# A held weight load and an earlier one: expert 1's second matrix waits for a store, expert 2's loads go out one group sooner

## The chip, the cores and the metric

The kernel runs on one core of a Trainium2 chip. The metric is the time of one execution on the device, in microseconds. Three runs of the kernel before took 1010.5, 1010.03 and 1009.81 us; their median is 1010.03 us.

The core has five engines, each of which takes its instructions in a fixed order: TensorE (PE, matmuls and transposes into the eight banks of PSUM), VectorE (DVE), ScalarE (ACT), GpSimd (POOL) and SyncE (SP, which here only issues transfers). Transfers go through 16 DMA engines, which two queues of this kernel feed at the same time: those that SP issues (the profile's q1, hardware_dynamic) and those that GpSimd issues (q0, software_dynamic).

## The reference

An attention with feature maps feeds a mixture of eight experts. Cut to what matters:

```python
def phi(x):
    proj = einsum('bhsd,df->bhsf', x, w_phi)
    proj = proj - max(abs(proj), axis=-1, keepdims=True)
    return concatenate([exp(proj), exp(-proj)], axis=-1)
q_p, k_p = phi(q), phi(k)
kv, z = einsum('bhsf,bhsd->bhfd', k_p, v), sum(k_p, axis=2)
x = (q_p @ kv) / (q_p @ z + 1e-06)          # then reshaped to 4608 x 512

P = exp(x @ w_gate - max)                    # 4608 tokens x 8 experts
for _ in range(8):
    P /= P.sum(1, keepdims=True) + 1e-09
    P /= P.sum(0, keepdims=True) + 1e-09
    P *= N / E
for e in range(8):
    out += P[:, e:e + 1] * (maximum(x @ w1[e], 0) @ w2[e])
```

Every token goes through every expert; w1[e] is 512 x 1024 and w2[e] 1024 x 512, each 2 MB in float32 and 1 MB in bfloat16 on the chip.

## The kernel before, in words

The program is written as a list of operations with what each reads, writes and which buffers it takes. A planner (class `Plan`, line 199) gives each engine its order: it models durations, buffers and both DMA queues (class `Links`, line 127, in which a transfer has a speed of its own and gets a share when both queues are busy), and starts whatever can start first; among operations that can start at the same moment the one written first goes first. The order that comes out is what the engines execute. So a change of a dependency, or of where a call stands in the text, can move instructions on every engine.

**Stages.** From 0 to about 204 us runs the attention. It leaves x in SBUF, transposed, as `xT`: 4608 tokens in nine groups of 512. Then run the routing (`routing`, line 1146: eight rounds that alternate on VectorE between row sums and column sums, with one small matmul against `colw` a round on TensorE, line 622 in the profile) and, at the same time on TensorE, the up and down products of expert 0. From about 244 us on come experts 1 to 7, whose products use Strassen-Winograd sums: seven products instead of eight, with sums of blocks formed beforehand on VectorE (`sub`, line 1236; all of these have line 1240 in the profile).

**Sums of x.** For expert 1 `sums_x` (line 1428) forms them per pair of groups: three sums X[3], X[2], X[4] and, because experts 2 to 7 use one more level for three of the products, `fine_x` (line 1365) forms four more for each of the blocks "11", "21" and "t1". All are stored to DRAM by SP: `xd` (X[n], line 1422), `xp` (a block that needs no sums, line 1450), and `xi` or `xi0t`, `xi2t`, `xi4t`, `xi6t` (the fine blocks; two parts straight from `xT`, lines 1369 and 1371, and the four sums in one store of 256 KB, line 1385). Experts 2 to 7 read them back (`load_fine`, line 1389).

The ring "X" has four buffers (line 492). X[3], X[2] and X[4] of the pair keep three of them until expert 1's product has read them. The fourth is taken in turn by the sums of "11", "21" and "t1" and then by the first sum of the next pair: VectorE can't write the next ones until the store of the last has landed. VectorE takes everything else, the rounds of the routing among it, behind these subtractions in its order. SP has eight semaphores for its transfers, used in turn, and so issues a transfer only when the eighth before it has landed.

**Weights.** `load_w` (line 514) has GpSimd issue two transfers, w1[e] and then w2[e], each 2 MB read and 1 MB written, with a cast. There are two places for each matrix: `wx`, which the attention uses until it ends, and one that expert 0 uses. Expert 1's loads wait for the key "late", the end of the attention. Those of expert e > 1 wait also for `("acc", 4, 0, 0)`: the first quarter of the accumulator of group 4, so that they stand on GpSimd behind the accumulation that writes it in the expert before. Expert 1's w2 is read by `sums_down`, called at the end of its second unit, and by its down products.

**The expert loop** (line 1979). Each expert goes through the pairs (0,1), (2,3), (4,5), (6,7) and the group 8. The down product of a group (`down7`, line 1791) runs in the units of the groups behind it. It forms sums of the hidden tile on VectorE (`hx<-hs`, line 1240), multiplies, and adds P times the result to `acc`: in part on VectorE (line 1860), in part on ScalarE (line 1872) and then GpSimd (line 1875, three accumulations for a group, in the order in which the down products come). `up7` (line 1480) finishes hidden tiles with an add and a relu on VectorE (line 1530 for expert 1) and on ScalarE (line 1535); one PSUM bank carries several products in turn, so that the next may start only when the add or read of the last is done.

Of the kernel before, what the change touches and what calls it, by code (L numbers as in the profile page):

```python
# [349 lines left out]
def kernel(  # L350
# [11 lines left out]
    nc = tc.nc  # L362
# [32 lines left out]
    acc = [accp.tile([128, 4, DD], FP32, name=f"acc{g}", tag=f"acc{g}") for g in range(NA)]  # L395
# [12 lines left out]
    late = {}  # L408
# [19 lines left out]
    def dma(queue, nbytes, rate, fn, r=(), w=()):  # L428

        speed, unit = LINK.get(rate, (rate, 40))  # L430
        if nbytes == 2 << 20:
            speed, unit = 400, 150
        o = plan.op(queue, 0.8 if queue == "POOL" else 0.6, 0.0, fn, r, w, (), nbytes / speed)
        o.turn, o.unit = rate == 148, unit

    TI, GR, KM, QM, PM, NM, RM = 0, 0, 0, 0, 0, 0, 0
    R = {}
# [68 lines left out]
    def new(tag):  # L506
        return R[tag].new()
# [3 lines left out]
        return buf().bitcast(BF16)  # L511


    def load_w(e, r=()):
        w1, w2 = new("w1"), new("w2")
        for w, src in ((w1, moe_w1), (w2, moe_w2)):
            dma("POOL", 2 << 20, 280, lambda w=w, src=src: nc.gpsimd.dma_start(
                out=w(), in_=src[e].rearrange("(c p) f -> p c f", p=128)),
                r, [(w, i, j) for i in range(2) for j in range(2)])
        return w1, w2  # L520

    def load_w0(i, r):
# [508 lines left out]
    for b in range(2):  # L1031
# [4 lines left out]
        w=["wphi_f0"])  # L1036
    dma("ACT", 1 << 15, 100, lambda: nc.scalar.dma_start(out=wphi_f[64:128, :], in_=w_phi),
        w=["wphi_f1"])
# [13 lines left out]
    for i in range(2):  # L1052
        dve(450, lambda i=i: nc.vector.memset(vrd[i], 0.0),
            w=[("vrd", i, h, *y) for h in range(2) for y in ((), (1,))])
# [79 lines left out]
    o = plan.op("X", 0.0, 0.0, swap, w=["late"])  # L1134
# [101 lines left out]
    def sub(eng, el, out_, x, y, op, r, w):  # L1236
        f = nc.vector if eng is dve else nc.gpsimd
        kw = {"shared": True} if eng is dve else {}
        eng(el * 0.5 if eng is dve else el * 1.04 + 128,
            lambda: f.tensor_tensor(out=out_(), in0=x(), in1=y(), op=op), r, w, **kw)  # L1240

    def sums_up(e, w1):

        def q(i, j):
            return lambda: w1()[:, 2 * j:2 * j + 2, 512 * i:512 * i + 512]

        S = [None] + [new("T") for _ in range(3)]

        def s(n):
            return lambda: S[n]().rearrange("p (a b) -> p a b", a=2)  # L1250


        a11, a12, a21, a22 = (1, 0), (1, 1), (0, 0), (0, 1)
        late = ["late"] + (["P"] if e == 1 else [])

        def k(a):
            return [(w1, *a)]

        sub(dve, 1024, s(2), q(*a11), q(*a21), ALU.subtract, k(a11) + k(a21) + late, [S[2]])
        sub(dve, 1024, q(*a21), q(*a21), q(*a22), ALU.add, k(a22) + late, k(a21))  # L1260
        sub(dve, 1024, s(1), q(*a21), q(*a11), ALU.subtract, k(a21) + k(a11) + late, [S[1]])
        sub(dve, 1024, s(3), q(*a12), s(1), ALU.subtract, k(a12) + [S[1]] + late, [S[3]])
        A = {"11": (q(*a11), k(a11)), "12": (q(*a12), k(a12)), "22": (q(*a22), k(a22)),
             "s1": (q(*a21), k(a21)), "s2": (s(1), [S[1]]), "s3": (s(2), [S[2]]),
             "s4": (s(3), [S[3]])}
        if e > 1:
            for n in INNER:
                fine_up(A, n)
        return A
# [48 lines left out]
    def xq(gs, i, j):  # L1318

        n = len(gs)  # L1320
        return lambda: xT[:, 2 * i:2 * i + 2, 512 * gs[0]:512 * (gs[0] + n)].rearrange(
            "p k (a b) -> p a k b", a=n)[:, :, :, 256 * j:256 * j + 256]

    def xall(gs):
        return [k for g in gs for k in xkeys(g)]
# [12 lines left out]
    class Turns:  # L1338
# [4 lines left out]
        def next(self):  # L1343
# [16 lines left out]
    Xi = {(g[0], n): dram.tile([128, 7, 256], BF16, name=f"xi{g[0]}{n}")  # L1360
          for g in pairs for n in INNER.values()}
# [3 lines left out]
    def fine_x(gs, n, b, r0):  # L1365

        g = gs[0]
        r = xall(gs) + ["late", *r0]
        dma("SP", 1 << 16, 160, lambda: nc.sync.dma_start(
            out=Xi[g, n][:, 0, :], in_=b()[:, 0, 0, :]), r, [("Xi", g, n, 0)])  # L1370
        dma("SP", 1 << 17, 160, lambda: nc.sync.dma_start(
            out=Xi[g, n][:, 1:3, :], in_=b()[:, :, 1, :]), r, [("Xi", g, n, 1)])
        y = new("X")

        def t(n):
            return lambda: y().rearrange("p a k c -> p (a k) c")[:, n]

        def blk(k, a):
            return lambda: b()[:, a, k, :]

        sub(dve, 256, t(0), blk(0, 1), blk(0, 0), ALU.subtract, r, [(y, 0), "order of X"])
        sub(dve, 256, t(2), blk(1, 1), blk(0, 1), ALU.subtract, r, [(y, 2)])
        sub(dve, 256, t(1), blk(1, 1), t(0), ALU.subtract, [*r, (y, 0)], [(y, 1)])
        sub(dve, 256, t(3), blk(1, 0), t(1), ALU.subtract, [*r, (y, 1)], [(y, 3)])
        dma("SP", 1 << 18, 160, lambda: nc.sync.dma_start(
            out=Xi[g, n][:, 3:7, :], in_=y().rearrange("p a k c -> p (a k) c")),
            [(y, i) for i in range(4)], [("Xi", g, n, 2)])

# [27 lines left out]
    def new_x():  # L1416
        return {n: new("X") for n in (2, 3, 4)}
# [10 lines left out]
    def sums_x(gs, r0=()):  # L1428

        X = new_x()  # L1430

        def x(n):
            return lambda: X[n]()[:, 0:len(gs)]

        b11, b12, b21, b22 = (xq(gs, *ij) for ij in ((0, 1), (0, 0), (1, 1), (1, 0)))
        el, keys = 512 * len(gs), xall(gs)
        r = keys + ["late", *r0]
        sub(dve, el, x(3), b22, b12, ALU.subtract, r, [X[3], "order of X"])
        sub(dve, el, b12, b12, b11, ALU.subtract, ["late", *r0], keys)
        sub(dve, el, x(2), b22, b12, ALU.subtract, r, [X[2]])  # L1440
        sub(dve, el, x(4), b21, x(2), ALU.subtract, r + [X[2]], [X[4], "order of X"])
        for n in (3, 2, 4):
            move_x(gs, n, True, X)
        if len(gs) == 2:
            for n, b in (("22", b22), ("11", b11), ("21", b21), ("t1", b12)):
                if n in INNER.values():
                    fine_x(gs, n, b, r0)
                else:
                    for a in range(2):
                        dma("SP", 1 << 17, 160, lambda n=n, a=a, b=b: nc.sync.dma_start(  # L1450
                            out=Xp[gs[0], n][:, a], in_=b()[:, a]), r, [("Xp", gs[0], n, a)])
        return X
# [524 lines left out]

    early, dn = [plain(8)], plain(7)
    for e in range(1, E):
        w1, w2 = load_w(e, ["late", ("acc", 4, 0, 0)] if e > 1 else ["late"])  # L1980
        if e == 1:
            nextX = sums_x(pairs[0])
        A7 = sums_up(e, w1)
        B7 = sums_down(e, w2) if e > 1 else None
        turn = [*pairs, (8,)] if e < E - 1 else [(8,), *pairs]
        if e == 2:
            o = plan.op("X", 0.0, 0.0, lambda: None, w=["K"])
            for d in plan.ops[:-1]:
                if any(b.ring is R["X"] for b in d.bufs):
                    d.users.append(o)  # L1990
                    o.deps.append(d)
                    o.left += 1
        for n, gs in enumerate(turn):
            if (e, n) == (1, 4):
                plan.inorder = 1
            X = nextX if e == 1 else load_fine(gs)
            H = {g: [] for g in gs}
            for fp in range(len(gs)):
                hs = take()
                for i, z in enumerate(hs):  # L2000
                    H[gs[min(i, len(gs) - 1)]].append(z)
                fine = e > 1 and len(gs) == 2
                if fine:
                    un = up49(A7, fp, X, H, gs, ["up0", "K"])
                else:
                    un = up7(A7, gs, fp, X, H, ["up0"])
                for o in UNITS[turns.pop(0)]:
                    if o in un:
                        un[o]()
                    elif len(o) == 3:  # L2010
                        un[o[:2], int(o[2])]()
                    elif dn is not None:
                        dn[o]()
                if dn is not None:
                    dn["out"]()
                    slots.extend(dn["slots"])
                if e == 1 and fp == 0 and n + 1 < len(turn):
                    nextX = sums_x(turn[n + 1], [(H[gs[0]][0], 0, 1, 1)])
                if B7 is None and fp:
                    B7 = sums_down(e, w2)  # L2020
                if fp == len(gs) - 1:
                    wait += [(e, g, H[g], B7, w2, [z.ring.number for z in H[g]]) for g in gs]
                dn = next_down()
# [35 lines left out]
```

## Time and profile before

| | us |
|---|---|
| median of 3 runs | 1010.03 |
| lowest and highest of them | 1009.81, 1010.5 |
| the profiled execution's own time | 1010.62 |
| its span in the profile | 1008.8 |
| attention, about | 0 to 204 |
| routing and the rest of expert 0, about | 204 to 244 |
| expert 1 (its units and sums), about | 244 to 349 |
| experts 2 to 7, about | 349 to 1004 |
| granted clock of TensorE | 1.0 in each stage |

The profile is of one execution; 1.8 us of its time lie outside the span. A row of the timeline gives start and length in us, engine, line, operation, tiles, the number of instructions merged into it, and in brackets how long the engine had been idle before and what ended that. A row "PE ps L622 <- DVE cs L1179: 0.4, 1, 0.4" of the waits says that TensorE waited for VectorE 0.4 us in all, once, at most 0.4 us. A row of the DMA issues gives the tiles, the queue, how many, KB each, and the us from issue to landing, that is until the semaphore which tells that it is done. A row of a DMA queue gives packets, MB and the time of those packets as a share of 16 engines.

### The profile page before, as it was taken

What the parts mean: (1) busy time and instruction counts of PE and PEld (TensorE: products, weight loads), DVE (VectorE), ACT (ScalarE), POOL (GpSimd) and SP (SyncE); (2) the same over time, 40 slices, a digit from 0 to 9 for tenths busy, and PEclk for the clock granted to TensorE, in tenths of its full rate; (3) what the DMA queues carried; (4) which work ended last, traced back from release to release, by engine and by line L of the source; (5) the groups of instructions that cost most, each with busy time, mean ns of one, the idle gap of its engine ahead of it and who ended that gap; (6) DMA issues with size and microseconds to landing.
All of it is one profiled execution on the core that took longest, in us unless ns stands there. A gap on an engine that the chain in (4) does not pass through costs nothing.

```text
span 1008.8 us, 23309 instructions
## 1 busy us (share of the span) xinstructions
PE 994.0 (99%) x8376; PEld 727.7 (72%) x8376; DVE 898.6 (89%) x1999; ACT 812.8 (81%) x1930; POOL 447.6 (44%) x514
## 2 busy tenths in 40 slices
PE   7899999999999999999999999999999999999998
PEld 5666666644566877777777877787778777787775
DVE  7999998987888998899989898989889988989886
ACT  7999999845979788878878788777887888778874
POOL 5778674400133344434444444444443444344443
PEclk9999999999999999999999999999999999999999
DMA  9999999181136423282327133632246222724653
GB/s 249 183 202 183 157 153 144 38 170 56 53 121 143 147 97 98 84 184 96 109 98 170 44 100 131 130 127 98 97 117 177 97 98 84 147 79 142 208 174 126
DMA packets 129748, 128.86 MB, mean 128 GB/s; under 512 B 55776, under 2 KB 98272, under 8 KB 129632
## 3 DMA queue, kind: packets, MB, share of 16 engines
q1 hardware_dynamic: 97680, 103.33, 36.3%
q0 software_dynamic: 31648, 23.86, 16.9%
q8 instruction: 65, 1.06, 0.5%
q14 instruction: 51, 0.42, 0.2%
q10 hardware_dynamic: 304, 0.20, 0.1%
HBM read 122.50 MB, written 19.53 MB: 141 GB/s over the span
## 4 chain that ended last, share of the span: by engine, by line
PE 92%; DVE 3%; ACT 2%; DMA 2%; issue 1%; POOL 0%; DVEq 0%
PE ps L1466 41%; PE ps L1475 20%; PE ps L622 17%; PE ps L1607 11%; PE ps L905 2%; DMA xi6t<-X 1%; DMA xi<-X 1%; PE ps L752 1%; ACT q L618 0%; DVE m L614 0%; ACT k L618 0%; DVE wx L614 0%; DVE X L1240 0%; DMA acc<-in_k_dram 0%; DVE hs L1676 0%
## 5 line engine op out<-in xcount | busy, mean ns | idle before, releaser
L1875 POOL TENSOR_TENSOR acc<-acc,hx 128x512 f32<-128x512 f32 x186 | 236.1, 1276 | 404.7 <-ACT hx L1872 135.0
L1466 PEld LDWEIGHTS <-hs 128*128 128x128 bf16 x1984 | 194.1, 98 | 46.4 <-issue 0.2
L1872 ACT ACTIVATE hx<-ps,P 128x256 f32<-128x256 f32 x372 | 158.9, 483 | 53.4 <-PE ps L1466 52.0
L1860 DVE SCALAR_TENSOR_TENSOR acc<-ps,P,acc 128x256 f32<-128x256 f32 x372 | 162.2, 478 | 30.2 <-PE ps L1466 28.2
L1475 PE MATMUL ps<-xT,T 128*128 128x512 bf16 x608 | 171.0, 379 | 0.0
L1466 PEld LDWEIGHTS <-hx 128*128 128x128 bf16 x1488 | 145.6, 98 | 24.9
L1466 PE MATMUL ps<-hx,hs 128*128 128x256 bf16 x992 | 144.3, 273 | 0.0
L1676 DVE CUSTOM_DVE_ANT_0 hs<-ps,U 128x512 bf16<-128x512 f32 x192 | 124.7, 684 | 11.3 <-PE ps L1475 6.6
L1607 PE MATMUL ps<-xT 128*128 128x256 bf16 x576 | 125.4, 272 | 0.0
L1475 PEld LDWEIGHTS <-T 128*128 128x128 bf16 x672 | 65.8, 98 | 40.6
L1682 ACT ACTIVATE hs<-ps 128x512 bf16<-128x512 f32 x96 | 55.9, 598 | 41.7 <-PE ps L1475 40.2
L1466 PE MATMUL ps<-wx,hs 128*128 128x256 bf16 x560 | 78.4, 273 | 0.0
L622 PE MATMUL ps<-w,hx 128*128 128x512 bf16 x288 | 73.0, 379 | 0.0
L622 PE MATMUL ps<-xT,w 128*128 128x512 bf16 x288 | 72.9, 379 | 0.0
L1466 PE MATMUL ps<-wx,hx 128*128 128x256 bf16 x496 | 72.3, 273 | 0.0
L1676 DVE CUSTOM_DVE_ANT_0 hs<-ps,X 128x512 bf16<-128x512 f32 x96 | 65.1, 684 | 7.8 <-PE ps L1607 6.9
L1466 PE MATMUL ps<-hx 128*128 128x256 bf16 x496 | 71.2, 273 | 0.0
L1607 PEld LDWEIGHTS <-xT 128*128 128x128 bf16 x576 | 56.3, 98 | 17.5
L1466 PE MATMUL ps<-w,hx 128*128 128x256 bf16 x432 | 62.2, 273 | 0.0
L614 DVE TENSOR_REDUCE m<-ps 128x4 f32<-128x512 f32 x88 | 58.8, 680 | 3.7 <-PE ps L622 1.9
L1672 ACT COPY X<-ps 128x512 f32<-128x512 f32 x96 | 58.6, 610 | 2.5 <-DVE ps L1650 2.5
L1466 PE MATMUL ps<-w,hs 128*128 128x256 bf16 x432 | 60.2, 273 | 0.0
(174 smaller groups left out, 2256.0 us busy)
## 6 DMA issues: line engine op xcount, KB each, us to landing
xT<-xi SPq DMA_DIRECT2D x48, 448.0 KB, 4.6
xT<-xd SPq DMA_DIRECT2D x72, 256.0 KB, 4.0
wx<-in_moe_w_dram POOLq DMA_DIRECT2D x8, 1024.0 KB, 11.2
v_m<-in_v_dram SPq DMA_DIRECT2D x15, 512.0 KB, 5.2
out_dram<-acc SPq DMA_DIRECT2D x14, 512.0 KB, 3.0
w<-in_moe_w_dram POOLq DMA_DIRECT2D x6, 1024.0 KB, 11.0
xT<-xp SPq DMA_DIRECT2D x24, 256.0 KB, 2.8
qk<-in_k_dram POOLq DMA_DIRECT2D x12, 256.0 KB, 5.4
```

Source lines behind the costliest of these rows:

```text
L614: dve(el, lambda: nc.vector.tensor_reduce(out=dst(), in_=src(), axis=AX.X, op=ALU.max, apply_absolute_value=True), r, w)
L622: nc.tensor.matmul(out_, lhsT=lhsT, rhs=rhs, start=start, stop=stop)
L905: pe(65, lambda j=j: nc.tensor.matmul(pn()[:, j * D1:j * D1 + D1], lhsT=s["T"][x]()[:, j % 2, 2 * h + j // 2, :] if j < 4 else r["T"][x]() ...
L1466: pe(256, lambda i=i, k=k, z=z: nc.tensor.matmul(bank()[:, 256 * i:256 * i + 256], lhsT=lhs(k, i), rhs=rhs(k), start=first and z, stop=k = ...
L1475: pe(512, lambda k=k: nc.tensor.matmul(bank().rearrange("p (a b) -> p a b", a=2), lhsT=lhs(k), rhs=rhs(k), start=first and k == 0, stop=k ...
L1607: pe(256, lambda: nc.tensor.matmul(halves_of(bank[q], n)(), lhsT=lhs(), rhs=t()[:, rhs, :], start=start, stop=True, skip_group_check=True) ...
L1672: act(512, lambda: nc.scalar.copy(out=flat(to[q])(), in_=bank[q]()), [bank[q]], [(to[q], 0), (to[q], 1)])
L1676: dve(515, lambda: nc.vector._custom_dve(ADD_SAT, out=out_(q, i, j), in0=bank[q]().rearrange("p (a b) -> p a b", a=2), in1=to[q](), s0=3.0 ...
L1682: act(512, lambda: nc.scalar.activation(out=out_(q, i, j), in_=bank[q]().rearrange("p (a b) -> p a b", a=2), func=ACT.Relu, bias=0.0, scal ...
L1860: dve(320, lambda n=n, ts=ts: nc.vector.scalar_tensor_tensor(out=acc[g][:, ts, 256 * j:256 * j + 256], in0=bank()[:, 256 * n:256 * n + 256 ...
L1872: act(370, lambda n=n: nc.scalar.activation(out=u()[:, n, :], in_=bank()[:, 256 * n:256 * n + 256], func=ACT.Copy, bias=0.0, scale=P[:, 4 ...
L1875: pool(695, lambda: nc.gpsimd.tensor_tensor(out=acc[g][:, 2 * i:2 * i + 2, 256 * j:256 * j + 256], in0=acc[g][:, 2 * i:2 * i + 2, 256 * j: ...
```

## The change

Three edits. `dma` returns its operation, and `fine_x` keeps that of its last store, by pair and block, in `written`. `load_w` gets a third argument, the key of a store: with it, the load of w2 is made to depend on that key in the plan, and on the chip it waits for that store (`behind`, which the planner turns into a dependency between the two instructions). Expert 1 passes the store of the "t1" sums of pair 0; the others pass none. For that, the call of `sums_x` for pair 0 now stands before that of `load_w`. And the loads of expert 2 wait for `("acc", 3, 0, 0)`, group 3 of expert 1, where they waited for group 4; experts 3 to 7 keep group 4.

```diff
         o = plan.op(queue, 0.8 if queue == "POOL" else 0.6, 0.0, fn, r, w, (), nbytes / speed)
         o.turn, o.unit = rate == 148, unit
+        return o
...
-    def load_w(e, r=()):
+    written = {}
+
+    def load_w(e, r, store):
         w1, w2 = new("w1"), new("w2")
-        for w, src in ((w1, moe_w1), (w2, moe_w2)):
-            dma("POOL", 2 << 20, 280, lambda w=w, src=src: nc.gpsimd.dma_start(
+        for w, src, behind in ((w1, moe_w1, None), (w2, moe_w2, store)):
+            o = dma("POOL", 2 << 20, 280, lambda w=w, src=src: nc.gpsimd.dma_start(
                 out=w(), in_=src[e].rearrange("(c p) f -> p c f", p=128)),
-                r, [(w, i, j) for i in range(2) for j in range(2)])
+                r + ([behind] if behind else []),
+                [(w, i, j) for i in range(2) for j in range(2)])
+            o.behind = written.get(behind)
         return w1, w2
...
-        dma("SP", 1 << 18, 160, lambda: nc.sync.dma_start(
+        written["Xi", g, n, 2] = dma("SP", 1 << 18, 160, lambda: nc.sync.dma_start(
             out=Xi[g, n][:, 3:7, :], in_=y().rearrange("p a k c -> p (a k) c")),
             [(y, i) for i in range(4)], [("Xi", g, n, 2)])
...
     for e in range(1, E):
-        w1, w2 = load_w(e, ["late", ("acc", 4, 0, 0)] if e > 1 else ["late"])
         if e == 1:
             nextX = sums_x(pairs[0])
+        r = ["late", ("acc", 3 if e == 2 else 4, 0, 0)] if e > 1 else ["late"]
+        w1, w2 = load_w(e, r, ("Xi", 0, "t1", 2) if e == 1 else None)
         A7 = sums_up(e, w1)
```

## The prediction

> **What bounds the kernel now.** I read the page first, then busy time by stage, then the waits of TensorE, then the chain of waits.
>
> ```profile
> span 1008.8 us, 23309 instructions
> ...
> PE 994.0 (99%) x8376; PEld 727.7 (72%) x8376; DVE 898.6 (89%) x1999; ACT 812.8 (81%) x1930; POOL 447.6 (44%) x514
> ```
>
> ```profile
> 200.00:244.00 44.00, 43.64 (x251) 20.53 (x250) 37.41 (x108) 18.02 (x32) 1.74 (x2) 1.00 0.48 104
> 300.00:340.00 40.00, 39.37 (x283) 27.45 (x282) 35.62 (x89) 34.43 (x70) 13.21 (x11) 1.00 0.75 195
> 340.00:440.00 100.00, 100.00 (x801) 78.12 (x799) 90.82 (x195) 82.11 (x204) 44.98 (x44) 1.00 0.33 89
> ```
>
> ```profile
> PE ps L622 <- DVE cs L1179: 0.4, 1, 0.4
> PE ps L1475 <- DVE hs L1530: 0.6, 1, 0.6
> ```
>
> ```profile
> 217.08 6.40 DMA xi<-X
> 317.00 7.75 DMA xi6t<-X
> ```
>
> TensorE sets the end. In the stage rows (start:end, length, then busy time of TensorE, its weight loads, VectorE, ScalarE, GpSimd) it lacks 0.36 us of 200 to 244, 0.63 us of 300 to 340 and nothing of the next 100. The two waits are those of the third fence, both on VectorE; and in the chain, each has a slow store of x sums behind it. These stages are the ones that the change touches. So the most it can give is 0.36 + 0.63 = 0.99 us, 0.1% of the span, while every microsecond by which VectorE newly holds up TensorE is lost for good: no later stage has slack to give it back.
>
> **Part one: expert 1's second load waits for the store.** The order of instructions shows two moves beside the wait. On GpSimd the load stands behind the store of the t1 sums of pair 0; nothing else is queued there until 269.95, when the first accumulation runs. On VectorE the planner, which expects the stores to land sooner, has pulled the subtractions for "21" from the fourth round of the routing into the third, and those for t1 from the fifth into the fourth. TensorE's column-sum matmuls of rounds 3 and 4 stand two matmuls later.
>
> ```profile
> 216.20 0.46 DVE L1167 TENSOR_TENSOR T<-L,rr 128x288 f32<-128x288 f32 x1
> ...
> 223.50 0.29 DVE L1240 TENSOR_TENSOR X<-xT 128x256 bf16<-128x256 bf16 x1 [1.49 <-DMA xi<-X]
> ...
> 226.89 0.66 DVE L1170 TENSOR_REDUCE cs<-T 128x8 f32<-128x288 f32 x1
> ```
>
> ```profile
> 228.10 16.38 PE ps L622 x78
> ```
>
> ```profile
> 218.03 0.18 PE L622 MATMUL ps<-cs,colw 128*128 128x24 bf16 x1
> ...
> 228.10 0.19 PE L622 MATMUL ps<-cs,colw 128*128 128x24 bf16 x1 [0.36 <-DVE cs L1179]
> ```
>
> ```profile
> q0 software_dynamic: 526, 1.04, 80.6%
> ...
> q1 hardware_dynamic: 228, 0.31, 11.8%
> ```
>
> ```profile
> q1 hardware_dynamic: 1075, 0.89, 88.0%
> ```
>
> The fourth X buffer, which "11", "21" and t1 share in turn, comes free when the "11" store lands: 217.08 + 6.40 = 223.48, and VectorE starts at 223.50 after 1.49 us of idling. In the new order VectorE is there right after T of round 3, at 216.69. When will that store land? The two queue rows above are of 204 to 212.4 us (packets, MB, share): by then the GpSimd queue has moved the first weight matrix (1.04 MB), and SP's queue 0.31 MB. SP's transfers up to and with the "11" store are 4 x 256, 2 x 128, 3 x 64 and 2 x 128 KB, 1.77 MB; 1.46 MB are left. From here on SP has the engines alone, as at 220 to 223, the last row: 0.89 MB in 3 us at 88%, so 0.34 MB a us. 1.46/0.34 = 4.3 us gives 216.7; a store on idle engines takes 2.0 us (a row of part two), of which its 0.26 MB need 0.8, so landing comes some 1.0 us after the bytes, at 217.7. VectorE then waits 1.0 us, in round 3. From that subtraction to the column matmul it takes about 1.5 us: 226.89 to 228.10 is 1.21 from the reduction on, with one subtraction inside, and of two more of 0.2 us one fits half into a gap. So the matmul can run at 219.2. TensorE takes 0.21 us a matmul here (16.38 us for 78), is there at 218.03 + 0.42 = 218.45 and waits 0.8 us. The old wait of 0.36 goes: sum +0.45 us. Ends: the store lands in time, -0.36; it takes from 215.0, when it can be issued, the whole 6.40 us, landing at 221.4, +4.1. I stay near the lower end, since the transfer behind those 6.40 us is the one that is held.
>
> ```profile
> 259.15 0.68 DVE L1240 TENSOR_TENSOR hx<-wx 128x1024 bf16<-128x1024 bf16 x1
> ```
>
> The held load itself I cost at nothing. The t1 store should be issued near 224 and, on idle engines, land 2 us later; the load then takes the 14.3 us of the slowest of its kind in the rows of part two at most, and is there by 241. VectorE reads the matrix first at 259.15. That cover of 18 us would have to go before it cost anything.
>
> **Part two: expert 2's loads go out two accumulations sooner.** On GpSimd they stood behind the 13th accumulation of expert 1 and now stand behind the 11th. VectorE's and SP's own orders are the same here.
>
> ```profile
> 310.01 1.27 POOL L1875 TENSOR_TENSOR acc<-acc,hx 128x512 f32<-128x512 f32 x1 [5.50 <-DVE hx L1240]
> ...
> 316.00 1.69 POOL L517 DMA_DIRECT2D w<-in_moe_w_dram  x2
> ```
>
> ```profile
> 312.40 0.32 SPq L1385 DMA_DIRECT2D xi<-X  x1
> 317.00 0.32 SPq L1385 DMA_DIRECT2D xi6t<-X  x1
> ```
>
> ```profile
> xi<-X SPq DMA_DIRECT2D x1, 256.0 KB, 2.0
> ...
> w<-in_moe_w_dram POOLq DMA_DIRECT2D x1, 1024.0 KB, 14.3
> xi6t<-X SPq DMA_DIRECT2D x1, 256.0 KB, 7.8
> ```
>
> ```profile
> 203.41 1.74 POOL L517 DMA_DIRECT2D wx<-in_moe_w_dram  x2 [7.21 <-PE ps L622]
> ...
> 204.54 0.35 SPq L1422 DMA_DIRECT2D xd<-X  x1
> ...
> xd<-X SPq DMA_DIRECT2D x1, 256.0 KB, 8.3
> ```
>
> ```profile
> q0 software_dynamic: 226, 0.46, 89.6%
> ```
>
> ```profile
> q0 software_dynamic: 371, 0.66, 89.1%
> q1 hardware_dynamic: 144, 0.26, 19.8%
> ```
>
> The third and fourth fences end in issues with KB and us to landing. A 256 KB store that is issued 1.00 us after a weight load (317.00 after 316.00) lands 7.75 us later, and one issued 1.13 us after (204.54 after 203.41) takes 8.3 us; the same store with no load near takes 2.0. The last two fences say why: from 317 to 321 the load's queue moves 226 packets and SP's queue not one, though its store was issued at 317.00; from 321 to 325 its 144 packets all go. A store that arrives just behind a fresh load waits some 4 us.
>
> Now the load goes out at 310.01 + 1.27 = 311.2 or so, and the "21" store of pair 6 at 312.40, 1.2 us behind it. So the slow store isn't avoided; it is another one, and a worse one to lose, since its buffer is wanted at 315.96 and not at 323.8. With 7.75 to 8.3 us it lands at 320.15 to 320.7; I take 320.3.
>
> ```profile
> 315.96 0.49 DVE L1240 TENSOR_TENSOR X<-xT 128x256 bf16<-128x256 bf16 x2
> ...
> 318.14 0.42 DVE L1240 TENSOR_TENSOR hx<-hs 128x512 bf16<-128x512 bf16 x1 [0.83 <-PE ps L1466]
> ...
> 320.31 0.88 DVE L1860 SCALAR_TENSOR_TENSOR acc<-ps,P,acc 128x256 f32<-128x256 f32 x2 [0.30 <-PE ps L1466]
> ...
> 321.70 0.87 DVE L1860 SCALAR_TENSOR_TENSOR acc<-ps,P,acc 128x256 f32<-128x256 f32 x2
> ...
> 324.77 0.42 DVE L1240 TENSOR_TENSOR X<-xT 128x512 bf16<-128x512 bf16 x1 [1.01 <-DMA xi6t<-X]
> ```
>
> ```profile
> 322.71 0.59 PE L1475 MATMUL ps<-xT,wx 128*128 128x512 bf16 x2
> ```
>
> ```profile
> 330.20 0.97 PE L1475 MATMUL ps<-X,wx 128*128 128x512 bf16 x3 [0.62 <-DVE hs L1530]
> ```
>
> VectorE stands at the t1 subtraction for 320.3 - 315.96 = 4.3 us. Behind it, in order, are the sums of the next down product, the adds that finish the hidden tiles, and the reads that empty PSUM banks. VectorE can make up the 0.83 and 0.30 us in which it had waited for TensorE. The reads of 321.70 end at 322.57, and the matmul of 322.71 takes the bank that they empty: TensorE has 0.14 us to spare there, and loses 4.3 - 1.1 - 0.1 = 3.1 us. Against this the old wait goes: VectorE's 1.01 us at 324.77 and TensorE's 0.62 at 330.20, with about 0.16 more inside that group (three matmuls in 0.97 us, where two take 0.59 and one more adds 0.22). TensorE, 3.1 us late, finds those adds done. Sum: 3.1 - 0.8 = +2.3 us. Landing at 320.15 makes it +2.1, at 320.7 +2.7. Were the store not slowed, VectorE would wait nowhere new and the sum lies between 0 and -0.8.
>
> What is late next is the t1 store of pair 6. It can go out at 321.3 and runs against the second matrix, whose load lands at about 311.2 + 0.8 + 14.3 = 326.3. With that queue empty I put it at 326.9, and VectorE, 4.3 - 1.1 = 3.2 us late, asks for the buffer at 323.8 + 3.2 = 327.0: no further cost. If it takes the 7.8 us again, to 329.1, 2.1 us more are lost. The first matrix is needed for sums at 326.46 by the old clock and lands well before; earlier loads gain nothing there. TensorE, ScalarE and VectorE stand in a slightly other order for some ten microseconds near 350; that row of 100.00 says no wait there now, and I count 0 with 0.3 us either way.
>
> [...]
>
> **The sum.** +0.45 and +2.3 make +2.75 us on the profiled execution of 1010.62 us, thus 1013.4 there. The runs shown have a median of 1010.03, so I forecast 1012.8 for theirs.
>
> **The rivals.** First, not slower: the "21" store gets its turn at once. The place is 312.40, the price is what TensorE loses at 322.71, and the point from which it decides is a landing before 317.1, for VectorE and TensorE together absorb 1.2 us after 315.96. If its 144 packets go between those of the load as in the row of 321 to 325, at most 3 us are added to 2.0 and it lands by 317.4: 0 to 0.3 us lost, and the t1 store then meets the load in its turn, as now. With part one, 1010.0 to 1010.8. For it: SP's queue does share once the load has run for 5 us. Against it: both stores that came 1.0 to 1.2 us behind a load were shut out.
>
> Second, it does what it seems made for: both slow stores vanish, TensorE waits nowhere, 1010.03 - 0.99 = 1009.0. For it: both waits in the chain are such stores, and the held load isn't there when "11" and "21" are written. Against it: in part one the first matrix alone holds SP's queue to 0.31 MB, and VectorE now asks five microseconds sooner.
>
> Third, worse: both stores of pair 6 are slow, one after the other. 2.75 + 2.1 = 4.9 us, 1014.9. For it: the t1 store does meet a running load. Against it: that load is then near its end.
>
> A rival that the held load comes too late for expert 1 has 18 us against it, and I give it nothing. That the change does nothing is excluded by the order on GpSimd.
>
> **How the numbers follow.** Forecast 0.68, with a range of its own of 1011.9 to 1013.8 (part one between 0 and +1.1, part two between +1.9 and +2.7); first rival 0.15, second 0.07, third 0.10. The range from 1010.2 to 1014.4 leaves out the second rival, a quarter of the first and most of the third, under 0.2. A difference of 0.2%, 2.0 us, is about what a measurement of this kernel can tell from no change. Slower by more than that (above 1012.05): nine tenths of the forecast and all of the third, 0.71. Faster by more is out of reach of the 0.99 us; 0.02 for what I have overlooked. The rest, 0.27, is the same.
>
> **What would show it.** Right: a new wait of VectorE of about 4 us for the "21" store of pair 6 near 316, with that store 7 to 9 us under way; TensorE idle some 3 us between 320 and 327, behind an add or a freed bank; the wait of 330 gone; a wait of about 0.8 us for the column sums in round 3. Wrong: that store landing before 317; TensorE with less than 1 us idle from 300 to 340; a first wait over 2 us in the routing, which would put the cost in part one; or a wait of VectorE for the held matrix near 259.

## The result and the profile after

| | before | after |
|---|---|---|
| median of 7 runs each, us | 1010.03 | 1013.66 |
| lowest and highest, us | 1009.62, 1011.17 | 1012.05, 1014.62 |
| profiled execution, us | 1010.62 | 1012.05 |
| its span, us | 1008.8 | 1010.3 |

The ratio is 1.0032, with a 95% interval of 1.0022 to 1.0042: the changed kernel is slower by 0.3%. The profiled execution of the kernel after is the fastest of its seven. The page of the kernel after begins so:

```profile
span 1010.3 us, 23274 instructions
...
PE 991.8 (98%) x8340; PEld 727.4 (72%) x8376; DVE 898.5 (89%) x1999; ACT 813.9 (81%) x1930; POOL 448.2 (44%) x514
```

The stages of the kernel after (columns as before: start:end, length, busy time of TensorE, its weight loads, VectorE, ScalarE and GpSimd, granted clock, DMA share, GB/s):

```profile
200.00:244.00 44.00, 43.58 (x244) 20.63 (x247) 37.60 (x107) 17.77 (x32) 1.72 (x2) 1.00 0.47 104
...
300.00:340.00 40.00, 37.62 (x268) 25.89 (x266) 34.24 (x88) 32.79 (x66) 12.19 (x10) 1.00 0.73 188
340.00:940.00 600.00, 599.69 (x4815) 470.70 (x4813) 541.00 (x1164) 480.96 (x1169) 262.81 (x250) 1.00 0.40 112
```

The first stage is as it was: TensorE lacks 0.42 us of 44 where it lacked 0.36. From 300 to 340 it lacks 2.38 us where it lacked 0.63, and the next 600 us give nothing back. The waits of TensorE from 200 to 340 in the kernel after:

```profile
PE ps L1480 <- DVE hs L1535: 2.2, 2, 1.4
PE ps L1480 <- DVE acc L1865: 0.2, 1, 0.2
PE ps L627 <- DVE cs L1184: 0.2, 1, 0.2
```

(The lines of the kernel after are 5 further down, that of the loads 3: L1480 is L1475 of before, L1535 is L1530, L1865 is L1860, L627 is L622, L1245 is L1240, L1390 is L1385, L520 is L517.) The wait for the column sums has shrunk to 0.2 us; the wait for the reads that empty the banks has grown from 0.6 to 2.2. The timelines of GpSimd, SP and VectorE, and of TensorE, show what is behind it:

```profile
310.59 1.69 POOL L520 DMA_DIRECT2D w<-in_moe_w_dram  x2
```

```profile
311.77 0.32 SPq L1390 DMA_DIRECT2D xi<-X  x1
320.80 0.32 SPq L1390 DMA_DIRECT2D xi6t<-X  x1
```

```profile
319.75 0.49 DVE L1245 TENSOR_TENSOR X<-xT 128x256 bf16<-128x256 bf16 x2 [4.34 <-DMA xi<-X]
...
326.09 0.43 DVE L1245 TENSOR_TENSOR X<-xT 128x512 bf16<-128x512 bf16 x1
```

```profile
322.77 0.59 PE L1480 MATMUL ps<-X,wx 128*128 128x512 bf16 x2 [1.40 <-DVE hs L1535]
324.15 0.59 PE L1480 MATMUL ps<-X,wx 128*128 128x512 bf16 x2 [0.79 <-DVE hs L1535]
```

The load goes out at 310.59 and the "21" store of pair 6 at 311.77, 1.18 us behind it. VectorE then stands for 4.34 us at the t1 subtraction, released by that store, and TensorE after it for 1.40 and 0.79 us. Two of the transfers in the chain of waits (start, length):

```profile
213.78 3.20 DMA xi<-X
...
311.77 7.89 DMA xi<-X
```

Before, these stood at 6.40 us ("11" store of pair 0) and 7.75 us (t1 store of pair 6). The first slow store has become shorter; the second has moved one store ahead, to "21". The queues in the kernel after, from 311 to 315 and from 315 to 319:

```profile
q0 software_dynamic: 191, 0.39, 70.6%
```

```profile
q0 software_dynamic: 310, 0.62, 84.7%
q1 hardware_dynamic: 142, 0.26, 20.4%
```

For the first four microseconds SP's queue moves no packet, although its store has been issued at 311.77; in the next four, 142 packets go. This is the picture that the prediction read from the trace of before, at another store.

### The profile page after: what moved, and what is told of

It reads as the page before. It is cut to its first block, busy times and chain, and to the rows that moved or that the text cites. A ratio compares the mean times of both kernels' runs of the same rounds, so it can differ in the third digit from the quotient of the medians.

```text
span 1010.3 us, 23274 instructions
## 1 busy us (share of the span) xinstructions
PE 991.8 (98%) x8340; PEld 727.4 (72%) x8376; DVE 898.5 (89%) x1999; ACT 813.9 (81%) x1930; POOL 448.2 (44%) x514
## 4 chain that ended last, share of the span: by engine, by line
PE 90%; DVE 3%; DMA 3%; ACT 3%; issue 1%; SPq 0%; DVEq 0%
PE ps L1471 41%; PE ps L1480 20%; PE ps L627 16%; PE ps L1612 11%; PE ps L910 2%; DMA xi<-X 1%; ACT q L623 1%; DMA xp<-xT 1%; ACT k L623 1%; DVE X L1245 1%; DMA acc<-in_q_dram 1%; DVE m L619 0%; DVE acc L1865 0%; DVE wx L619 0%; DVE hs L1535 0%
## 5 line engine op out<-in xcount | busy, mean ns | idle before, releaser
L1865 DVE SCALAR_TENSOR_TENSOR acc<-ps,P,acc 128x256 f32<-128x256 f32 x372 | 162.1, 477 | 29.7 <-PE ps L1471 27.8
L1480 PE MATMUL ps<-xT,T 128*128 128x512 bf16 x608 | 171.1, 379 | 0.0
L1480 PEld LDWEIGHTS <-T 128*128 128x128 bf16 x672 | 65.8, 98 | 40.7 <-issue 0.3
L627 PE MATMUL ps<-xT,w 128*128 128x512 bf16 x271 | 70.2, 379 | 0.6
L627 PE MATMUL ps<-w,hx 128*128 128x512 bf16 x275 | 69.9, 379 | 0.5
```

The source lines that it names most:

```text
L627: nc.tensor.matmul(out_, lhsT=lhsT, rhs=rhs, start=start, stop=stop)
L1480: pe(512, lambda k=k: nc.tensor.matmul(bank().rearrange("p (a b) -> p a b", a=2), lhsT=lhs(k), rhs=rhs(k), start=first and k == 0, stop=k ...
L1865: dve(320, lambda n=n, ts=ts: nc.vector.scalar_tensor_tensor(out=acc[g][:, ts, 256 * j:256 * j + 256], in0=bank()[:, 256 * n:256 * n + 256 ...
```

## The experiments

The kernel before ran beside each set: 1010.29 us for e1 to e4 (27 runs), 1010.25 for e5 to e8 (17), 1010.17 for e9 and e10 (15).

**e1: part one alone.**

```diff
-        r = ["late", ("acc", 3 if e == 2 else 4, 0, 0)] if e > 1 else ["late"]
+        r = ["late", ("acc", 4, 0, 0)] if e > 1 else ["late"]
```

> Part one alone: expert 1's second matrix is held behind the t1 store of pair 0, expert 2's loads stay behind group 4. My theory: the t1 store of pair 6 is slow again (about 7.8 us) and TensorE waits about 0.6 us near 330 as before, while the '21' store of pair 6 lands in 2.0 us; in the routing TensorE waits 0 to 0.4 us where it waited 0.36. So the time is that of the kernel before, 1009.6 to 1010.5. Rival (part one costs something, for instance at the column sums of round 3 or where VectorE asks for the held matrix): 1011.5 or more, with TensorE idle over 1 us between 200 and 262.

Measured: 1010.14 us, ratio 0.9999 (0.9990 to 1.0008). The stage row and TensorE's waits:

```profile
300.00:340.00 40.00, 39.25 (x278) 26.96 (x276) 35.83 (x91) 34.31 (x70) 12.56 (x10) 1.00 0.74 194
```

```profile
PE ps L1480 <- DVE hs L1535: 0.7, 1, 0.7
PE ps L627 <- DVE cs L1184: 0.2, 1, 0.2
```

From 300 to 340 it is the kernel before, with the t1 store of pair 6 slow (7.87 us in the chain). Part one costs nothing that can be measured.

**e2: part two alone**, the kernel before with one line changed.

```diff
-        w1, w2 = load_w(e, ["late", ("acc", 4, 0, 0)] if e > 1 else ["late"])
+        w1, w2 = load_w(e, ["late", ("acc", 3 if e == 2 else 4, 0, 0)] if e > 1 else ["late"])
```

> Part two alone: expert 2's loads stand behind the 11th accumulation, expert 1's second matrix is not held. My theory: the '21' store of pair 6 takes 7.5 to 8.5 us, VectorE waits about 4 us for it, TensorE is idle 2.2 to 3.1 us between 300 and 340, and the time is 1.5 to 3.6 us above the kernel before, that is as much as the whole change. Rival (the cost is in part one): within 0.7 us of the kernel before.

Measured: 1013.53 us, ratio 1.0030 (1.0018 to 1.0042).

```profile
300.00:340.00 40.00, 37.33 (x265) 25.71 (x264) 33.93 (x87) 32.46 (x66) 12.21 (x10) 1.00 0.73 189
```

```profile
PE ps L1475 <- DVE hs L1530: 2.5, 2, 1.7
PE ps L1475 <- DVE acc L1860: 0.2, 1, 0.2
```

The whole loss is here: 2.67 us idle, and a time like that of the full change.

**e3: the changed kernel with expert 2's loads behind the 12th accumulation.**

```diff
-        r = ["late", ("acc", 3 if e == 2 else 4, 0, 0)] if e > 1 else ["late"]
+        r = ["late", ("acc", 3, 2, 1) if e == 2 else ("acc", 4, 0, 0)] if e > 1 else ["late"]
```

> The changed kernel with expert 2's loads behind the 12th accumulation instead of the 11th; every engine's order is otherwise the same. They go out near 313.3, about 1.5 us behind the '21' store of pair 6 and 3 us ahead of its t1 store. My theory (a store is shut out when it arrives just behind a load): the '21' store lands in 2.0 us, VectorE does not wait near 316, TensorE's idle time from 300 to 340 falls below 1 us, and the time is 2 to 4 us below the changed kernel, 1009.2 to 1010.8. Rival (the load slows whatever SP moves while it runs, so that an earlier load costs by its length and not by its place): within 1 us of the changed kernel.

Measured: 1009.59 us, ratio 0.9996 (0.9987 to 1.0005). The stage row, the issue of the loads, and the DMA issues from 312 to 319 (KB each, us to landing):

```profile
300.00:340.00 40.00, 40.00 (x288) 27.89 (x286) 37.04 (x91) 35.21 (x72) 13.33 (x11) 1.00 0.75 196
```

```profile
314.51 1.68 POOL L520 DMA_DIRECT2D w<-in_moe_w_dram  x2
```

```profile
xi<-X SPq DMA_DIRECT2D x1, 256.0 KB, 2.0
xi6t<-X SPq DMA_DIRECT2D x1, 256.0 KB, 6.2
```

One place later on one queue, and TensorE isn't idle at all from 300 to 340. The "21" store is now 1.35 us ahead of the loads and takes 2.0 us; the t1 store, 3.90 us behind them, takes 6.2 us, which VectorE has time for. The ratio's interval holds 1: this run alone shows the loss gone, not yet a gain.

**e4: the changed kernel once more**, without an edit.

> The changed kernel once more, for the spread of its runs and a second profile. If one fixed wait makes the cost, TensorE's idle time from 300 to 340 is 2.2 to 2.6 us again and the times lie within 0.7 us of each other. If the cost depends on how the transfers happen to meet, the times spread over 2 us again (1012.0 to 1014.7) and the second profile shows another sum of waits than the first.

Measured: 1013.84 us, ratio 1.0033 (1.0022 to 1.0045). Neither branch of the expectation fits: the idle time of TensorE from 300 to 340 is the same as in the first profile of this kernel (2.41 and 2.38 us), and yet the times spread over 2.8 us, and the span of the profiled execution is 1011.9, 1.6 us more. The stretches of 2 us of e4, and then those of the first profile (the last columns are granted clock, DMA share and GB/s):

```profile
320.00:322.00 2.00, 1.93 (x14) 1.19 (x13) 1.05 (x5) 2.00 (x5) 0.00 (x0) 1.00 1.21 199
322.00:324.00 2.00, 0.07 (x1) 0.06 (x1) 2.00 (x6) 0.56 (x1) 0.58 (x1) 1.00 1.24 207
324.00:326.00 2.00, 1.60 (x4) 0.43 (x4) 2.00 (x6) 0.60 (x1) 1.92 (x2) 0.50 0.90 217
326.00:328.00 2.00, 2.00 (x7) 0.74 (x6) 2.00 (x6) 1.33 (x3) 0.04 (x1) 0.65 0.05 14
328.00:330.00 2.00, 2.00 (x12) 0.98 (x10) 2.00 (x7) 2.00 (x5) 0.00 (x0) 1.00 0.19 66
```

```profile
322.00:324.00 2.00, 0.59 (x2) 0.19 (x2) 2.00 (x5) 0.61 (x2) 1.66 (x2) 1.00 1.24 209
324.00:326.00 2.00, 1.66 (x7) 0.67 (x7) 2.00 (x5) 0.99 (x2) 0.88 (x1) 1.00 0.52 157
326.00:328.00 2.00, 2.00 (x11) 0.93 (x10) 1.99 (x7) 2.00 (x5) 0.00 (x0) 1.00 0.20 66
```

In e4 the clock is at one half from 324.0 on: all of the row from 324 to 326, and of the next, with a mean of 0.65, 2 x (1 - 0.65) / 0.5 = 1.4 us. That makes 3.4 us at half speed, thus 1.7 us of work lost: the 1.6 us between the two spans. In the 3.4 us ahead of the fall TensorE was busy only for 0.07 us from 322 on and about 1.3 us before. The first profile, with its idle time in pieces of 1.40 and 0.79, has a clock of 1.00 throughout. In e4 a wait of 2.4 us thus cost 4.

**e5: only the first of the two loads goes early.** The second is held behind the 13th accumulation.

```diff
-        w1, w2 = load_w(e, r, ("Xi", 0, "t1", 2) if e == 1 else None)
+        w1, w2 = load_w(e, r, {1: ("Xi", 0, "t1", 2), 2: ("acc", 4, 0, 0)}.get(e))
```

> The changed kernel, but of expert 2's two loads only the first goes out behind the 11th accumulation; the second stays behind the 13th, as before the change. Only GpSimd's order differs, by that one issue. Theory (a store issued 1.0 to 1.2 us behind a fresh weight load is shut out, however much is queued after it): the 21 store of pair 6 still takes 7.5 to 8.3 us, TensorE still idles 2 to 2.6 us between 300 and 340, 1012.5 to 1014 us. Rival (the two matrices queued together, 2.1 MB, hold the store back): it takes 3 to 5 us, TensorE idles under 0.7 us there, 1009.6 to 1010.6 us.

Measured: 1013.37 us, ratio 1.0035 (1.0023 to 1.0047). The issue on GpSimd, the DMA issues from 311 to 314, the stage row and the largest wait:

```profile
311.59 0.79 POOL L520 DMA_DIRECT2D w<-in_moe_w_dram  x1
```

```profile
w<-in_moe_w_dram POOLq DMA_DIRECT2D x1, 1024.0 KB, 9.9
xi<-X SPq DMA_DIRECT2D x1, 256.0 KB, 8.1
```

```profile
300.00:340.00 40.00, 37.38 (x246) 24.22 (x244) 32.19 (x81) 31.87 (x63) 9.34 (x9) 0.96 0.67 161
```

```profile
PE ps L1480 <- DVE hs L1535: 2.4, 2, 1.6
```

One load is enough: the store, issued at 312.76, takes 8.1 us, though the second matrix wasn't queued before 316.36. The rival falls: the store's first packet goes at 316.77, 4.0 us behind its issue, and for 3.6 of these nothing is queued behind the load in front.

**e6: part two alone, at the 12th accumulation** (the edit of e3 in the kernel of e2, so nothing is held).

```diff
-        w1, w2 = load_w(e, ["late", ("acc", 4, 0, 0)] if e > 1 else ["late"])
+        w1, w2 = load_w(e, ["late", ("acc", 3, 2, 1) if e == 2 else ("acc", 4, 0, 0)] if e > 1 else ["late"])
```

> The kernel before with only part two, and that at the 12th accumulation instead of the 11th; expert 1's second matrix isn't held. Theory (only the distance of the loads from the two stores of pair 6 counts there): neither store of pair 6 holds up TensorE, which idles under 0.3 us from 300 to 340; the wait of 0.36 us for the column sums stays; 1009.5 to 1010.2 us, within 0.1% of the kernel with the hold. Rival (the hold is needed for the gain of that kernel): as the kernel before or slower, 1010.3 to 1011.5 us.

Measured: 1009.18 us, ratio 0.9993 (0.9984 to 1.0001). In its trace the "21" store is out 1.35 us before the load (311.83 and 313.18) and lands in 2.0 us, and TensorE lacks 0.01 us from 300 to 340. The hold isn't needed for the time of e3. The time is 0.3 us below what was expected, and the wait for the column sums, expected to stay, isn't among TensorE's waits of this trace.

**e7 and e8: two more profiles, for the granted clock**, of e2's kernel and of the changed kernel, both without a further edit.

> Part two alone once more, for one more look at the granted clock. Theory (a TensorE idle stretch that is near or over 2 us makes the granted clock fall to one half for about 3.4 us, a shorter one doesn't): a stretch up to 1.7 us goes with a clock of 1.0 and a span near 1009.7, one of 2.0 us or more with 0.5 for 3.4 us and a span 1.6 us or so longer. Rival (the fall is a chance event that isn't tied to the gap): falls elsewhere too, or none behind a gap of 2 us or more.

> The changed kernel once more, for one more look at the granted clock. As for the look before: an idle stretch of 2.0 us or more between 320 and 325 with a clock of 0.5 behind it for about 3.4 us and a span near 1012, or one of 1.7 us or less with a clock of 1.0 and a span near 1010.3. Rival: clock and gap don't go together.

Measured: 1013.11 us with a span of 1011.3 (e7) and 1014.37 with 1012.6 (e8), one run each. The stage row of e7 and that of e8:

```profile
300.00:340.00 40.00, 37.31 (x253) 24.82 (x251) 32.81 (x83) 31.32 (x63) 10.55 (x10) 0.96 0.68 172
```

```profile
300.00:340.00 40.00, 36.94 (x247) 24.23 (x245) 32.20 (x81) 31.02 (x61) 9.85 (x9) 0.96 0.67 166
```

Both clocks fell, behind a longest wait of 1.9 and 2.1 us. The six profiles of kernels with the slow "21" store, beside each other (the last column is explained below the table):

| profile | span, us | TensorE idle 300 to 340 | its longest wait | clock there | busy share of the emptiest window |
|---|---|---|---|---|---|
| first of after | 1010.3 | 2.38 | 1.4 | 1.00 | 0.59 |
| e2 | 1009.7 | 2.67 | 1.7 | 1.00 | 0.50 |
| e5 | 1013.0 | 2.62 | 1.6 | 0.96 | 0.37 |
| e7 | 1011.3 | 2.69 | 1.9 | 0.96 | 0.29 |
| e4 | 1011.9 | 2.41 | 2.0 | 0.96 | 0.41 |
| e8 | 1012.6 | 3.06 | 2.1 | 0.96 | 0.35 |

The fall and the idle stretch go together: it came in four of these six profiles and at this place in none of the other kernels' (before, e1, e3, e6, e9 and e10). But the threshold near 2 us of my expectation doesn't hold: e5 fell with 1.6 us and e2 didn't with 1.7. (Two profiles hold a fall in the attention too: e5 from 39.5 to 42.9, e3 from 13.8 to 17.2.)

What parts these six is where the idle time lies. Each trace records at which moments the clock changed, and within a trace they lie whole multiples of 3.413 us apart: in e5 the falls at 39.52 and 326.24, for instance, 84 of them. So in these traces the clock changes at the ends of windows of that length, and their place differs from execution to execution (in the first profile they are counted back from the fall at 1009.31, behind TensorE's last work: 201 of them to 323.23). Here are the window ahead of the fall in e5 and that behind it, then the window ahead of e4's fall, and the emptiest one in e2 and in the first profile (start:end, length, busy time of TensorE and the others, clock):

```profile
322.83:326.24 3.41, 1.25 (x5) 0.45 (x5) 3.41 (x9) 1.00 (x3) 2.52 (x2) 1.00 1.09 192
326.24:329.66 3.42, 3.42 (x9) 1.21 (x9) 2.67 (x7) 2.10 (x4) 0.00 (x0) 0.50 0.27 80
```

```profile
320.59:324.00 3.41, 1.40 (x12) 0.93 (x10) 3.05 (x10) 1.97 (x4) 0.58 (x1) 1.00 1.24 207
```

```profile
319.73:323.14 3.41, 1.72 (x13) 1.04 (x11) 3.38 (x11) 1.96 (x4) 0.61 (x1) 1.00 1.25 209
```

```profile
319.82:323.23 3.41, 2.01 (x14) 1.17 (x12) 3.38 (x11) 2.19 (x4) 0.97 (x1) 1.00 1.24 207
```

In all four falls TensorE was busy for 0.29 to 0.41 of the window just ahead; where the same idle time was shared out between two windows, leaving 0.50 or more in each, the clock stayed.

**e9: both loads of expert 2 held behind the t1 store of pair 6**, at group 4.

```diff
-        for w, src, behind in ((w1, moe_w1, None), (w2, moe_w2, store)):
+        for w, src, behind in ((w1, moe_w1, store if e == 2 else None), (w2, moe_w2, store)):
...
-        r = ["late", ("acc", 3 if e == 2 else 4, 0, 0)] if e > 1 else ["late"]
-        w1, w2 = load_w(e, r, ("Xi", 0, "t1", 2) if e == 1 else None)
+        r = ["late", ("acc", 4, 0, 0)] if e > 1 else ["late"]
+        w1, w2 = load_w(e, r, {1: ("Xi", 0, "t1", 2), 2: ("Xi", 6, "t1", 2)}.get(e))
```

> Part one as it is; expert 2's loads back at group 4, both of them held behind the t1 store of pair 6 as expert 1's second is behind that of pair 0. Theory (the slow stores are all that the loads cost here, and the price of holding is that the first matrix comes late): no store of pair 6 takes over 3 us; the first matrix goes out near 320 and lands near 330, while its sums were read from 326.5 on, so VectorE finds a wait of some us there or the planner has moved the sums; TensorE idles 0 to 2 us in 300 to 345; 1009.0 to 1011.5 us. Rival (a load held behind the stores is free, as in part one): no idling, 1009.0 to 1009.6 us.

Measured: 1016.33 us, ratio 1.0062 (1.0049 to 1.0074).

```profile
300.00:340.00 40.00, 40.00 (x295) 28.57 (x293) 34.37 (x83) 34.75 (x71) 13.92 (x11) 1.00 0.70 180
340.00:380.00 40.00, 35.44 (x275) 26.49 (x272) 32.57 (x74) 27.56 (x66) 14.39 (x14) 1.00 0.24 77
```

All stores of pair 6 land in 2 us and TensorE is never idle from 300 to 340, as expected; but it lacks 4.56 us of the next 40, outside both expectations. There it waits for ScalarE (1.1, 1.0, 0.8 in two parts, and 0.6 us the largest). The planner has put the order of the work around the start of expert 2 differently, because the loads come later in the plan; how much of the 4.56 us is that order and how much the late matrix was not separated.

**e10: the kernel of e6 once more.**

> The loads of expert 2 behind the 12th accumulation, nothing held, once more beside fresh runs of the kernel before. If that place is worth the 0.6 us by which the two stores of pair 6 held up TensorE, the ratio is 0.9990 to 0.9998 again and both sets together exclude 1. Rival (no gain, chance): 0.9998 to 1.0006.

Measured: 1008.97 us, ratio 0.9988 (0.9979 to 0.9997). The ratio is lower than expected, and this set alone excludes 1; that of e6 just didn't. The kernel of e6 beats both: by about 0.1%, or 1 us, it is faster than the kernel before. Its gain near pair 6 isn't whole each time: in this profile, of the slowest of the 11 runs, the t1 store takes 6.9 us, VectorE waits 0.80 us for it, and TensorE lacks 0.41 us from 300 to 340.

## Why the prediction was right, and where it wasn't

**The mechanism of part two was as predicted.** The prediction had the load going out at 311.2, the "21" store 1.2 us behind it, landing after 7.75 to 8.3 us, and VectorE waiting 4.3 us. Measured: 1.18 us behind, 7.89 us, 4.34 us. That excludes the first rival, in which the store gets its turn. The third, both stores slow, is out too: the t1 store was issued at 320.80 and took 5.3 us, and VectorE used its buffer at 326.09 without a wait, within a microsecond of the prediction. And e3 and e6, which put the store ahead of the loads, take the whole loss away.

**What TensorE loses to it was close.** In the first profile the "21" store goes out at 311.77 instead of 312.40, so that everything is 0.63 us earlier when part two begins. That is in the main the spread between executions: 0.31 us of it are there when expert 1's first load goes out (203.10 and 203.41), up to which VectorE, ScalarE and GpSimd have the same order in both kernels, and e2, without part one, is at the same store 0.95 us early (311.45). The same group of four matmuls, in the timeline of before and then of after:

```profile
324.43 1.03 PE L1475 MATMUL ps<-X,T 128*128 128x512 bf16 x4
```

```profile
326.66 1.03 PE L1480 MATMUL ps<-X,T 128*128 128x512 bf16 x4
```

326.66 + 0.63 - 324.43 = 2.86 us late, where 3.1 was predicted; TensorE was stopped one group earlier than the text said: not at the group of 322.71 but at the one ahead of it, which starts at 322.77 here. The old wait near 330 is gone, worth the 0.78 us that were put on it. Net +2.08, for +2.3 predicted; with the 0.63 us this is 2.08 - 0.63 = +1.45, and the two profiled executions differ by 1012.05 - 1010.62 = 1.43. Clear of that spread it is the 2.08 that part two costs in waits.

**Part one was mis-sized.** +0.45 was predicted, and e1 gives 0.9999 (0.9990 to 1.0008). The timeline of VectorE in the kernel after:

```profile
217.00 0.29 DVE L1245 TENSOR_TENSOR X<-xT 128x256 bf16<-128x256 bf16 x1 [0.66 <-DMA xi<-X]
```

The "11" store landed at 216.98, not 217.7. Of these 0.7 us, 0.31 are the earlier start of this execution. The rest comes from the 1.0 us that the prediction put between the last bytes and the landing, which is too much: the rate of 0.34 MB a us held (SP's queue moved 1.53 MB from 212.09 to 216.6), but a landing comes some 0.4 us behind the bytes. In e3 the "21" store is issued at 313.16, its packets start from 313.97 to 314.8, and it lands 2.0 us after its issue; so most of the 1.2 us beside the bytes passes ahead of the first packet. VectorE waited 0.66 us instead of 1.0 and TensorE 0.2 instead of 0.8, less than the 0.36 of before. The held load came at no cost, as predicted: issued at 226.01, it took 9.6 us, with its first reader at 258.52.

**The step that failed is that the sum ended with the waits.** It counted what TensorE stands idle and has no term for the clock, which is 1.0 in each stage row of before. In four of the six profiles the idle stretch brought a second price, 3.4 us at half clock. The times of e2's nine runs part accordingly: four from 1011.47 to 1011.95, with a mean clock of 0.999 or 1.0 over the run, and five from 1013.53 to 1015.97, all with 0.998; 1.7 us of 1010 are 0.0017. The two groups are 3.0 us apart, though, more than one such fall; the mean clock doesn't tell where it fell, and the other 1.3 us are not explained. So the total of +2.75 us was near the measured +3.6 in part by luck: one term too high (part one, +0.45 for about 0), one a little high (+2.3 for 2.08) and one missing (1.7). Between single executions, without a fall the change costs 1.4 us in the first profile, with it 3.1 in e4's (1013.73) and 3.75 in e8's. e8's 1014.37 stand against the 1010.62 of before; its idle time of 3.06 us is 2.43 above 0.63, its first stage lacks 0.12 more (43.52 of 44), and the fall adds 1.7, together 4.2; the 0.5 us between lie in the rest of the span.

**The second rival** (both slow stores vanish, 1009.0) did not happen in this change, but e6 comes to it near pair 6, and e10 in part: 1009.18 and 1008.97 us. These medians are 1.07 and 1.20 us below those of before, a little over the bound of 0.99 us on any gain; the intervals (up to 1.6 and from 0.3 to 2.1) leave the bound possible. Of it, 0.63 us lie near pair 6, and one place on one queue can give these; where the rest of the two gains comes from is not shown.

## What to carry to other kernels

A load that is moved earlier need not leave a collision behind; here it met the next small transfer on another queue, and what counted was which of them came first and by how much, and whose buffer was wanted soonest. Look for the place just behind the small transfer's issue: here one accumulation (2 to 3 us) decided between a loss of 0.3% and a gain of 0.1%. And when TensorE is the bound, price a new idle stretch of 2 us, as an estimate from these runs, at up to twice its length, by the clock that may follow it: 2.4 to 3.1 us of idle time cost another 1.7 in four of six profiles.

## What the runs showed of the hardware

**A store beside a running weight load waits for its first packet, longest behind a fresh load.** By the distance of the store's issue behind the load's, for the 256 KB stores of pair 6: 1.0 to 1.2 us behind, 7.75 to 8.6 us to landing (before, after, e1, e2, e4, e5, e7, e8); 3.9 us behind, 6.2 to 6.9 us (e3, e6, e10); 10.2 us and more, 5.3 us (after, e2, e4, e7, e8; in e5, where the second load is only 5.7 us ahead, 6.0); 1.35 us ahead, 2.0 us (e3, e6, e10). The later stores don't share at once either. In e3 the t1 store is issued at 318.41, and SP's queue moves nothing until 322.2:

```profile
q0 software_dynamic: 336, 0.68, 107.0%
```

From issue to first packet it is 4.0 to 4.5 us in the first group, 3.7 to 3.8 in the second, 2.5 to 3.2 in the third and 0.8 in the last; the rest of the difference lies behind the first packet. It doesn't take a second load queued behind the first (e5). A load's own first packet goes 1.5 us behind its issue. So I estimate, from these 1.5 us less the store's 0.8, that a store issued up to some 0.7 us behind a load would still be first; no run has that distance.

From the load's first packet to the first packet of that store, 257 to 279 packets of the load start in the eight traces of the first group (271 from 317.5 to 321.5 in that of before, 279 from 312.1 to 316.0 in that of after), 504 to 507 in e3 and e6, and 454 in e10. What sets these counts is not shown.

**The granted clock fell to one half for 3.4 us in four of the six profiles with the slow "21" store, each time behind a window of 3.4 us in which TensorE was mostly idle.** The windows of e4, e5, e2 and the first profile are shown above. The moments of the change lie whole multiples of 3.413 us apart, and each of the four falls lasts one such length (326.24 to 329.66 in e5). The window need not be idle throughout: no idle stretch of these six from 300 to 340 was longer than 2.1 us, and ahead of the four falls TensorE was busy for 0.29 to 0.41 of the window; with 0.50 and 0.59 (e2, first profile) the clock stayed. One window is out of line: in e3, in the attention, the clock fell behind one from 10.42 to 13.83 in which TensorE was busy for 0.60. So the busy share of the window goes with the fall in these six profiles, but does not settle it in every case.
